# Two attentions on one core: outputs kept with tokens in rows, and turned by DMA in the last stage

## The chip, the core and the metric

The kernel runs on one core of a Trainium2 chip. The core has five engines with a queue of instructions each: TensorE (PE in the profile, with its weight loads as PEld), VectorE (DVE), ScalarE (ACT), GpSimd (POOL) and SyncE (SP), which here issues every DMA. Each queue is worked in order; semaphores tie the queues together. The metric is the device time of one execution in microseconds, the median of several runs.

## The reference

Two attention layers over 2048 tokens of width 1024 with 32 heads of 32 stand side by side; their outputs are concatenated. Cut to what is computed:

```python
def _A_ref(x, wq, wk, wv, wo, beta):          # four segments of 512 tokens
    for s in range(N):
        p = _softmax(q_s @ k_s.T * scale + mask)
        a_dot = p @ v_s
        a_mem = phi(q_s) @ M / (phi(q_s) @ z + 1e-6)
        outs.append(g * a_mem + (1 - g) * a_dot)
        M, z = M + phi(k_s).T @ v_s, z + phi(k_s).sum(tokens)
    return concat(outs) @ wo
def _B_ref(x, wqkv, w_phi, wo):               # linear attention, all tokens
    phi(t) = concat(softmax(t @ w_phi), softmax(-t @ w_phi))
    o = phi(q) @ (phi(k).T @ v) / (phi(q) @ phi(k).sum(tokens) + 1e-6)
    return o @ wo
return concatenate([_A_ref(...), _B_ref(...)], axis=-1)
```

All of it is in 32-bit floats, so the kernel splits most operands into a high and a low half float ("halves") and multiplies three times: high x high, high x low, low x high.

## The kernel before

**Stages.** First comes attention A in 32 units (`attend`, `produce`), one for each segment and group of four heads; B's folded weights are prepared beside it. Then come B's keys and values (eight pairs of 128 tokens, by Strassen's scheme with seven products in place of eight), then B's queries with B's output projection (`project`, 16 blocks of 128 tokens), and last A's output projection, again by Strassen's scheme: eight passes `c`, each for the token blocks c and c + 8.

**A's outputs.** A unit ends with `osum`, a tile with 128 tokens in rows and, for each of four token blocks, 128 columns of four heads. TensorE turns the four 128x128 blocks (line 1108) into a bank of PSUM, ScalarE copies them to `oT` (line 676), and SP stores `oT` to the DRAM tensor `oa_d` (line 1110). So `oa_d` holds features in rows and tokens in columns. `oT` is also the name under which folded weights are kept on their way to DRAM (lines 534, 535 and 1135).

**The last stage.** A pass loads its two token blocks from `oa_d` (line 1686; tiles `e`, or S9 for pass 0), forms four sums and differences on VectorE (line 1692), and makes halves of seven operands: A11, A12, S1, S2, S4, S3, A22 (lines 455 and 457). The halves go to `ot`, `pt` and `h3` tiles, for pass 0 (`own`) to S15 and S8. They are the stationary operand of the matmuls (line 1725), 12 for each of the seven products, so 84 to a pass; the moving operand is one of seven forms of the output weights (S0 to S3, S10, S13, S14). Results leave through ScalarE (line 1742), VectorE (line 1749) and SP (line 1751); pass 0 keeps them in S12. The last product of the last pass leaves in two halves of its width (lines 1773, 1775 and 1778).

**Buffers by name.** S4 to S7 hold the halves of B's output weights (`bo`: S4 and S5 for the first 512 columns, S6 and S7 for the second) until the last `project` (line 428 with `misc<-S,ot`). The DMA transposes already there are at line 904 (keys of A) and line 1653 (B's queries: four for each block of 128 tokens, 128x1024 half floats each).

**The order.** Nothing is issued as written. Every operation goes into a graph with an expected duration, a priority and the operations it depends on, and `Graph.run` fills the five queues from it, always taking the operation with the best priority among those that could start by its own model of time. `nudge` shifts priorities by a pseudo-random amount that a table, `NUDGE`, sets for each stretch of 60 operations (`G.places` counts them). Where the model sees TensorE idle for long it puts in dummy matmuls (`fill`, line 386).

Of the kernel before, what the change touches and what calls it, by code (L numbers as in the profile page):

```python
# [8 lines left out]
F32 = mybir.dt.float32  # L9
F32R = mybir.dt.float32r  # L10
F16 = mybir.dt.float16
# [31 lines left out]
         ((3, 0, "subtract"), 3, 2), ((2, 3, "subtract"), 2, 6))  # L43
EUP = 2.0 ** 15
STRETCH, REACH = 60, (0.3, 0.7, 1.5, 3.0)
NUDGE = {0: 820989, 2: 102852, 3: 529656, 4: 266905, 5: 924189, 6: 435410, 9: 911235, 12: 450738, 13: 124130, 14: 669972,
# [15 lines left out]


def view(t, off, ap):
# [41 lines left out]
class Graph:  # L106
# [37 lines left out]
    def op(self, eng, dur, fn, r=(), w=(), prio=0, lat=0.0, short=False, port=False, need=(), kb=256, free=False):  # L144
        o = Op()
        o.short, o.port = short, port or eng == "POOL"
        o.eng, o.dur, o.fn, o.prio, o.lat, o.kb = eng, dur, fn, (prio, len(self.ops)), lat, kb
        o.banks = []
        ends, starts = set(), set()
        for b in need:  # L150
            if b.prev[0] is not None:
                ends.update(b.prev[0].ops)
        for write, accs in ((0, r), (1, w)):
            for acc in accs:
                b, key = acc if isinstance(acc, tuple) else (acc, None)
                b = b.of if type(b) is Part else b
                old, last, opened = b.prev
                if old is not None:
                    ends.update(old.ops)
                if not b.ops and last is not None:  # L160
                    starts.add(last.ops[0])
                if opened is not None:
                    starts.add(opened)
                for k in (list(b.writer) if key is None else [key, None]):
                    if k in b.writer:
                        ends.add(b.writer[k])
                if write:
                    for k in (list(b.readers) if key is None else [key, None]):
                        ends.update(b.readers.pop(k, ()) if k == key or key is None else b.readers.get(k, ()))
                    if key is None:  # L170
                        b.writer.clear()
                    b.writer[key] = o
                else:
                    b.readers.setdefault(key, []).append(o)
                b.ops.append(o)
                if b.kind is not None and b not in o.banks:
                    o.banks.append(b)
                    b.left += 1
        ends.discard(o)
        o.deps = [(d, 0) for d in ends] + [(d, 1) for d in starts - ends if d is not o]  # L180
        o.base, o.at = prio, None if free else self.places
        self.places += not free
        last = self.ops[-1] if self.ops else o
        if o.eng == "PE" and (last.eng, last.base, last.fn.__code__, last.banks) == (o.eng, prio, fn.__code__, o.banks):
            o.at = last.at
        o.prio = (prio + (0.0 if o.at is None else nudge(o.at)), len(self.ops))
        self.ops.append(o)
        return o
# [121 lines left out]
def tile_kernel(ctx: ExitStack, tc: tile.TileContext, ax, aw, awv, awo, beta, bx, bwqk, bwv, bphi, bwo, out):  # L310
# [97 lines left out]
    def bank(tag, shape, line=None):  # L408
        b = G.bank(tag, shape, F32, line or tag)
        psums.add(b)  # L410
        return b
# [263 lines left out]
    def copy(dst, src):  # L675
        return lambda: nc.scalar.activation(dst(), src(), AF.Copy)
# [241 lines left out]
    def attend(u):  # L918
# [5 lines left out]
        def pe(dur, fn, **kw):  # L924
            op(PE, dur, fn, prio=P, **kw)

        def act(dur, fn, **kw):
            op(ACT, dur, fn, prio=P, **kw)
# [173 lines left out]
        if s > 0:  # L1102
            pool(1.23, lambda: nc.gpsimd.tensor_tensor(
                osum(), osum(), amem().rearrange("p c h d -> p c (h d)"), op=OP.add), r=[amem, osum], w=[osum])
        oT = G.buf("a", [128, 4, 128], F32, "oT", 1)
        po = bank("misc", [128, 4, 128], "output")
        for i in range(4):
            pe(0.112, lambda i=i: nc.tensor.transpose(po()[:, i, :], osum()[:, i, :], ident), r=[osum], w=[po], need=[oT])
        act(0.48, copy(oT, po), r=[po], w=[oT])
        op(SP, 0.6, lambda: nc.sync.dma_start(oa_d[4 * s:4 * s + 4, :, g, :].rearrange("c p t -> p c t"), oT()),  # L1110
           r=[oT], w=[(osc, u)], prio=P, lat=1.5)

    wfb, xfb, bob = (G.fixed(t) for t in (wf_d, xf_d, bo_d))
    lanes = [G.fixed(None) for _ in range(2)]
# [561 lines left out]
    for c in range(NT // 2):  # L1676
# [18 lines left out]
        def half(t, h, o=0):  # L1695
            return lambda: t()[:, o + h]
# [5 lines left out]
        if own:  # L1702
            fb = [G.buf("slot", [128, 4096], F16, s) for s in ("S15", "S8")]
            at2 = [(fb[j // 4], j % 4) for j in range(7)]
        else:
            o2 = [G.buf("b", [128, 2112], F16, "ot", 4) for _ in range(2)]
            p2 = G.buf("b", [128, 2112 - 64], F16, "pt", 3)
            hx = G.buf("slot", [128, 2048], F16, "h3", 2)
            at2 = [(o2[0], 0), (o2[0], 1), (o2[1], 0), (o2[1], 1), (p2, 0), (p2, 1), (hx, 0)]

        def pick(t, i, a):
            return t()[:, 1024 * i + 512 * a:1024 * i + 512 * a + 512].rearrange("p (b c) -> p b c", c=128)

        for (f, src, k), (t, i) in zip((("A11", A0, 0), ("A12", A0, 1), ("S1", ss, 0), ("S2", ss, 1), ("S4", ss, 3),
                                        ("S3", ss, 2), ("A22", A1, 1)), at2):
            form[f] = (t, i, lambda a, t=t, i=i: pick(t, i, a))
            hl = [(t, (i, a), lambda a=a, t=t, i=i: pick(t, i, a)) for a in range(2)]
            sk = (src, k) if src is ss else (src, int(f == "A22"))
            halves(*hl, (sk, half(src, k, off if f == "A22" else 0)), (oscs, 0, lambda: osc2[:, 0]), 512, P)

        def mult(ps, f, w, start):
            t, i, v = form[f]
# [4 lines left out]
                        stop=(n == 3 and a == 1), skip_group_check=True),  # L1727
                       r=[(t, (i, a)), (wform[w], (b, n))], w=[ps], prio=P)

        kept = []  # L1730
        if own:
            ks = G.buf("slot", [128, 4, 512], F32, "S12")

        def keep(ps, tag, bufs):
            if own:
                t, i = ks, len(kept)
                kept.append(i)
                v = lambda: ks()[:, i]
            else:
                t, i = G.buf("b" if tag == "ez" else "stage", [128, 512], F32, tag, bufs), None  # L1740
                v = t
            op(ACT, 0.587, lambda: nc.scalar.activation(v(), ps(), AF.Copy, scale=wsc[:, 2, 1, 0:1]),
               r=[ps, (wscs, (2, 1))], w=[(t, i)], prio=P)
            return (t, i), v
# [74 lines left out]
```

## Time and profile before

| what | value |
|---|---|
| median of 3 runs | 1662.68 us (1659.73 to 1662.96) |
| the profiled execution | 1660.7 us |
| its span, first to last instruction | 1658.7 us |
| mean granted TensorE clock | 0.999 |
| attention A | to about 887 us |
| B's keys and values | about 887 to 1200 us |
| B's queries and `project` | about 1200 to 1509.7 us |
| A's output projection, passes 0 to 7 | 1509.7 to 1658.7 us |

The page's first row gives the busy time of each engine, and its second part the same in 40 slices of the span. A view by stretch gives, for each window, the length, the busy time of each engine with its number of instructions, the granted TensorE clock, the share of time the 16 DMA engines worked, and GB/s. A group of instructions is one line, engine and operation with its tiles, its count, busy time, mean duration in ns, and the idle time of its engine just before. A row of the timeline is start, duration, engine, line, operation, tiles, and count; SPq is SP's queue issuing DMAs. Rows of one line or tile end with the shortest, median and longest duration in ns. A row of waits reads: who waited, for whom, us in total, times, longest.

### The profile page before, as it was taken

The numbers are of one execution on the slowest core, as the hardware profiler recorded it, in microseconds if no ns is written. First come the engines' busy times: TensorE is split into PE (matmuls) and PEld (weight loads), VectorE is DVE, ScalarE is ACT, GpSimd is POOL, SyncE is SP. The second block draws the span as 40 slices with busy tenths as digits, with TensorE's granted clock in tenths as the row PEclk, the third lists the DMA queues.
The fourth block names the chain that finished last, engine by engine and source line by source line (L and its number), as shares of the span: only waits on it lengthen the run. The fifth ranks groups of instructions, "written<-read, shape, count | busy, mean of one in ns | idle before, by whom it ended". The sixth has DMA issues, their size and how long they took to land.

```text
span 1658.7 us, 35573 instructions
## 1 busy us (share of the span) xinstructions
PE 1639.3 (99%) x12922; PEld 967.3 (58%) x12922; DVE 1356.5 (82%) x3213; ACT 1110.3 (67%) x2044; POOL 1058.9 (64%) x1394
## 2 busy tenths in 40 slices
PE   9999999999999999999999999999999999999999
PEld 7666667667676666766754444445544444444444
DVE  6999989899887888897877898979996786975441
ACT  8799779869787777687865767645656464444331
POOL 4967577577787887967875444646799897640000
PEclk9999999999999999999999999999999999999999
DMA  7855556789556573766576364276466665763311
GB/s 239 239 139 154 155 161 171 202 206 248 110 158 163 136 186 88 196 193 181 164 215 228 121 222 147 96 272 241 169 152 143 174 174 152 221 149 133 121 57 64
DMA packets 265599, 279.68 MB, mean 169 GB/s; under 512 B 162768, under 2 KB 216016, under 8 KB 256848
## 3 DMA queue, kind: packets, MB, share of 16 engines
q1 hardware_dynamic: 265424, 277.42, 58.1%
q8 instruction: 101, 1.65, 0.4%
q14 instruction: 74, 0.61, 0.1%
HBM read 143.34 MB, written 85.00 MB: 138 GB/s over the span
## 4 chain that ended last, share of the span: by engine, by line
PE 76%; DVE 10%; POOL 6%; ACT 4%; issue 3%; DMA 0%; SPq 0%; POOLq 0%; ACTq 0%; DVEq 0%
PE proj L428 25%; PE proj L624 13%; PE misc L428 8%; PE proj L1725 5%; PE s L1040 3%; PE s L947 3%; PE pv L1076 3%; PE s L624 3%; PE s L1725 2%; PE misc L624 2%; PE misc L1725 1%; POOL e L1630 1%; DVE mx L1326 1%; PE pv L1661 1%; DVE ph L1047 1%
## 5 line engine op out<-in xcount | busy, mean ns | idle before, releaser
L428 PE MATMUL proj<-S,S 128*128 128x512 f16 (+1 forms) x2304 | 493.9, 343 | 0.8 <-DVE ph L1047 0.4
L428 PEld LDWEIGHTS <-S 128*128 128x128 f16 x3072 | 288.9, 98 | 158.0 <-ACT S L455 0.7
L624 PE MATMUL proj<-S,S 128*128 128x512 f16 x1488 | 342.8, 379 | 7.0 <-ACT cs L630 6.0
L624 PEld LDWEIGHTS <-S 128*128 128x128 f16 x1968 | 186.9, 98 | 220.3 <-issue 8.6
L1053 POOL TENSOR_SCALAR_AFFINE_SELECT ph<-ph 128x256 f16<-128x256 f16 (+1 forms) x448 | 194.3, 457 | 108.2 <-DVE ph L1047 91.3
L1047 DVE SCALAR_TENSOR_TENSOR ph<-s,ph 128x512 f16<-128x512 f32 x320 | 208.6, 684 | 49.4 <-ACT ph L1046 45.0
L953 DVE CUSTOM_DVE_ANT_0 s<-s,causal 128x384 f32<-128x384 f32 (+3 forms) x512 | 241.4, 511 | 7.4 <-PE s L947 4.8
L1046 ACT ACTIVATE ph<-s 128x512 f16<-128x512 f32 x320 | 184.8, 645 | 0.7
L428 PE MATMUL misc<-S,ot 128*128 128x512 f16 x768 | 171.0, 379 | 0.0
L1333 ACT ACTIVATE e<-e,sk 128x256 f32<-128x256 f32 x256 | 114.2, 497 | 60.7 <-DVE e L1330 38.9
L428 PEld LDWEIGHTS <-ot 128*128 128x128 f16 x768 | 73.9, 98 | 88.3
L1044 ACT ACTIVATE s<-s,bdl 128x512 f32<-128x512 f32 x160 | 105.6, 701 | 19.6 <-PE s L1040 19.6
L1044 ACT ACTIVATE s<-s,bd 128x512 f32<-128x512 f32 x160 | 102.9, 687 | 18.6 <-PE s L1040 16.9
L1040 PE MATMUL s<-S 104*128 104x512 f16 (+3 forms) x512 | 113.2, 299 | 0.3 <-ACT S L977 0.3
L947 PE MATMUL s<-S 96*128 96x512 f16 (+3 forms) x512 | 112.0, 299 | 0.7 <-DVE dm L1000 0.3
L428 PE MATMUL proj<-wv,S 128*128 128x256 f16 x768 | 101.1, 272 | 0.0
L1076 PEld LDWEIGHTS <-ph 128*128 128x128 f16 x2560 | 88.9, 96 | 19.1 <-POOL ph L1053 0.9
L1630 POOL TENSOR_TENSOR e<-e,zb 128x512 f32<-128x512 f32 x64 | 84.9, 1341 | 16.2 <-DVE r L1336 13.2
L1076 PE MATMUL pv<-vl,ph 128*128 128x66 f16 (+1 forms) x2560 | 92.5, 184 | 0.1
L1336 DVE TENSOR_REDUCE r<-e 128x32 f32<-128x1024 f32 x64 | 76.7, 1207 | 12.2 <-ACT e L1333 11.9
L624 PE MATMUL s<-S,S 128*128 128x512 f16 x324 | 78.6, 379 | 0.4 <-DVE S L457 0.4
L953 DVE DVE_READ_ACCUMULATOR2_ANT mt<- 128x1 f32 x512 | 72.7, 142 | 0.0
(376 smaller groups left out, 3302.4 us busy)
## 6 DMA issues: line engine op xcount, KB each, us to landing
S<-h SPq DMA_DIRECT2D x192, 128.0 KB
S<-wf_d SPq DMA_DIRECT2D x21, 1024.0 KB
st<-bwqk SPq DMA_DIRECT2D x56, 256.0 KB
wf_d<-fo SPq DMA_DIRECT2D x48, 256.0 KB
out<-os SPq DMA_DIRECT2D x38, 256.0 KB
wf_d<-oT SPq DMA_DIRECT2D x36, 256.0 KB
S<-xf_d SPq DMA_DIRECT2D x9, 1024.0 KB
S<-aw SPq DMA_DIRECT2D x16, 512.0 KB
```

Source lines behind the costliest of these rows:

```text
L428: op(PE, dur, lambda c=c, a=a, b=b, lv=lv, rv=rv: nc.tensor.matmul(pv(), lv(), rv(), start=(c == 0 and a + b == 0), stop=(c == n - 1 and a ...
L624: op(PE, 0.2165, lambda n=n, a=a, b=b, lv=lv, rv=rv: nc.tensor.matmul(ps(), lv(), rv(), start=(start and n == 0 and a + b == 0), stop=(n = ...
L947: nc.tensor.matmul(ps()[:, o:o + 128 * i + 128], st()[0:96, 0, h, 128 * i:128 * i + 128], st()[0:96, 1, h, 0:128 * i + 128], start=True, s ...
L953: dve({128: 0.216, 256: 0.381, 384: 0.6, 512: 0.648}[n], lambda h=h, i=i, o=o, n=n: nc.vector.tensor_tensor_reduce(ps()[:, o:o + n], ps()[ ...
L1040: nc.tensor.matmul(ps()[:, o:o + n], st()[0:104, 1, h, 128 * j:128 * j + 128], st()[0:104, 0, h, 128 * j:512], start=True, stop=True)
L1044: act(0.571, lambda: nc.scalar.activation(ps(), ps(), AF.Exp, bias=0.0, scale=bd()[:, 4, i2, 0:1]), r=[(bd, i2)], w=[ps])
L1046: act(0.478, lambda: nc.scalar.activation(ph()[:, 0], ps(), AF.Copy, scale=2.0 ** 14), r=[ps], w=[(ph, 0)])
L1047: dve(0.6, lambda: nc.vector.scalar_tensor_tensor(ph()[:, 1], ps(), 2.0 ** 14, ph()[:, 0], op0=OP.mult, op1=OP.subtract), r=[ps, (ph, 0)], ...
L1053: nc.gpsimd.affine_select(pd, pd, pattern=[[0, n], [1, 128]], compare_op=OP.is_ge, fill=0.0, base=0, channel_multiplier=-1)
L1076: nc.tensor.matmul(ps()[:, i, n0:n1], ph()[:, a, o:o + 128], vl()[:, j, h4 + h, n0:n1], start=(i == 0 and a == 0), stop=(j == min(i, 2)), ...
L1333: op(ACT, 0.41, lambda i=i: nc.scalar.activation(e()[:, 4 * i:4 * i + 4], e()[:, 4 * i:4 * i + 4], AF.Exp, bias=0.0, scale=sk()[:, i:i + 1 ...
L1725: op(PE, 0.2165, lambda n=n, a=a, b=b: nc.tensor.matmul(ps(), v(a)[:, n, :], wform[w]()[:, b, n, :], start=(start and n == 0 and a + b == ...
```

## The change

`oa_d` now holds A's outputs as the unit leaves them, tokens in rows. The four transposes, the bank of PSUM, and the copy to `oT` are gone, and SP stores `osum` itself. In the last stage the loads, the sums and differences, and the halves have the same shapes as before, with tokens in rows; then a DMA transpose turns each operand's halves (128 x 1024 half floats, high and low together), and the matmuls read the turned tiles. There are seven for each pass, 56 in all. The turned tiles are S12 and two `h3` tiles for pass 0, and by turns S6 and S7 (odd passes) and S4 and S5 (even passes) for the others, four operands in the first and three in the second. Since S12 is taken, pass 0 keeps its results in `cs` tiles. `G.places += 5` keeps the count of operations for the nudges; the transposes are not counted. The table `NUDGE` is another one, from its third entry on.

```diff
-NUDGE = {0: 820989, 2: 102852, 3: 529656, 4: 266905, 5: 924189, 6: 435410, 9: 911235, 12: 450738, 13: 124130, 14: 669972,
+NUDGE = {0: 820989, 2: 102852, 3: 733272, 5: 984992, 6: 222437, 8: 980432, 9: 306119, 10: 758093, 11: 242234, 12: 151133, 13:
...
-        oT = G.buf("a", [128, 4, 128], F32, "oT", 1)
-        po = bank("misc", [128, 4, 128], "output")
-        for i in range(4):
-            pe(0.112, lambda i=i: nc.tensor.transpose(po()[:, i, :], osum()[:, i, :], ident), r=[osum], w=[po], need=[oT])
-        act(0.48, copy(oT, po), r=[po], w=[oT])
-        op(SP, 0.6, lambda: nc.sync.dma_start(oa_d[4 * s:4 * s + 4, :, g, :].rearrange("c p t -> p c t"), oT()),
-           r=[oT], w=[(osc, u)], prio=P, lat=1.5)
+        G.places += 5
+        op(SP, 0.6, lambda: nc.sync.dma_start(oa_d[4 * s:4 * s + 4, :, g, :].rearrange("c p t -> p c t"), osum()),
+           r=[osum], w=[(osc, u)], prio=P, lat=1.5)
...
+        turned = [("S12", 4), ("h3", 2), ("h3", 1)] if own else [(f"S{4 + 2 * (c % 2)}", 4), (f"S{5 + 2 * (c % 2)}", 3)]
+        turned = [(b, k) for b, n in ((G.buf("slot", [128, 2 if t == "h3" else 4, 2, 4, 128], F16, t, 2 if t == "h3" else 1), n)
+                                      for t, n in turned) for k in range(n)]
...
-            form[f] = (t, i, lambda a, t=t, i=i: pick(t, i, a))
+            form[f] = (b, o, lambda a, b=b, o=o: b()[:, o, a])
             hl = [(t, (i, a), lambda a=a, t=t, i=i: pick(t, i, a)) for a in range(2)]
             sk = (src, k) if src is ss else (src, int(f == "A22"))
             halves(*hl, (sk, half(src, k, off if f == "A22" else 0)), (oscs, 0, lambda: osc2[:, 0]), 512, P)
+            op(SP, 1.24, lambda t=t, i=i, b=b, o=o: nc.sync.dma_start_transpose(
+                b()[:, o].rearrange("p a g t -> p (a g) t"), t()[:, 1024 * i:1024 * i + 1024]),
+               r=[x[:2] for x in hl], w=[(b, (o, a)) for a in range(2)], prio=P, lat=2.0, kb=256, free=True)
...
-            if own:
-                t, i = ks, len(kept)
-                kept.append(i)
-                v = lambda: ks()[:, i]
-            else:
-                t, i = G.buf("b" if tag == "ez" else "stage", [128, 512], F32, tag, bufs), None
-                v = t
+            t, i = G.buf(*CS) if own else G.buf("b" if tag == "ez" else "stage", [128, 512], F32, tag, bufs), None
+            v = t
```

What stands in the queues now, at three places. The first is TensorE in the attention: before, around the first unit's transposes (the rows that begin with L1108; `S_440` are A's key and query weights, `S_130` a unit's stacked keys and queries).

```order
L1013 LDWEIGHTS pkt
L1013 MATMUL misc<-vl_122,pkt 128x132
L1108 MATMUL misc<-ident,osum 128x128 x4
L428 LDWEIGHTS S_440
L428 MATMUL proj<-S_826,S_440 128x512
L428 LDWEIGHTS S_440
L428 MATMUL proj<-S_826,S_440 128x512
```

After the change no such row is left on TensorE, 32 times four transposes fewer, and SP's queue has the store of `osum` in the place of that of `oT`, between the copies of weights and halves of the units that follow:

```order
L885 DMA S_138<-h_1407 32x4x512 x2
L1136 DMA wf_d<-oT 1024x1x128
L1111 DMA oa_d<-osum 128x4x128
L1136 DMA wf_d<-fo 1024x1x128
L885 DMA S_138<-h_1407 32x4x512 x3
```

What moved: the four transposes went from TensorE, and the store waits for `osum` rather than for ScalarE's copy.

The second place is SP's queue at the entry to the last stage after the change. `out<-os` are the last results of `project`, S_21426 and S_21449 the turned tiles of pass 2 (in S4 and S5), S_21466 and S_21504 those of pass 1 (in S6 and S7), `cs` the results of pass 0.

```order
L1548 DMA out<-os 128x512
L1724 DMA_TRANSPOSE S_21426<-ot 128x8x128
L1548 DMA out<-os 128x512
L1724 DMA_TRANSPOSE S_21426<-ot 128x8x128
L1724 DMA_TRANSPOSE S_21449<-pt 128x8x128 x2
L1724 DMA_TRANSPOSE S_21466<-ot 128x8x128
L1548 DMA out<-os 128x512
L1724 DMA_TRANSPOSE S_21466<-ot 128x8x128 x3
L1724 DMA_TRANSPOSE S_21504<-pt 128x8x128
L1548 DMA out<-os 128x512
L1724 DMA_TRANSPOSE S_21504<-pt 128x8x128
L1724 DMA_TRANSPOSE S_21426<-ot 128x8x128 x2
```

New here are twelve transposes between the stores, with those for pass 2 ahead of those for pass 1. On TensorE, 17 of pass 0's 84 matmuls now stand in front of the last matmul of `project`, against one before.

The third place is SP's queue in a later pass. Before, it holds only the loads of `e` and the stores:

```order
L1751 DMA out<-st 128x512
L1686 DMA e<-oa_d 128x1024
L1751 DMA out<-st 128x512
L1751 DMA out<-ez 128x512
L1751 DMA out<-os 128x512
```

After, the stores of the passes ahead stand between the transposes of passes 4 and 5 (S_21839 and S_21905 are pass 4's turned tiles, S_21967 four operands of pass 5):

```order
L1724 DMA_TRANSPOSE S_21839<-ot 128x8x128 x4
L1750 DMA out<-st 128x512
L1750 DMA out<-ez 128x512
L1687 DMA e<-oa_d 128x1024
L1724 DMA_TRANSPOSE S_21905<-pt 128x8x128 x2
L1750 DMA out<-os 128x512
L1724 DMA_TRANSPOSE S_21905<-h_21675 128x8x128
L1750 DMA out<-st 128x512
L1724 DMA_TRANSPOSE S_21967<-ot 128x8x128 x3
```

What moved: seven transposes for a pass were put between the stores, so that a transpose can stand behind a store whose result is not there yet.

More of the change, by code (lines that the diff above doesn't have):

```diff
@@ L1709, in tile_kernel @@
             at2 = [(o2[0], 0), (o2[0], 1), (o2[1], 0), (o2[1], 1), (p2, 0), (p2, 1), (hx, 0)]
+        turned = [("S12", 4), ("h3", 2), ("h3", 1)] if own else [(f"S{4 + 2 * (c % 2)}", 4), (f"S{5 + 2 * (c % 2)}", 3)]
+        turned = [(b, k) for b, n in ((G.buf("slot", [128, 2 if t == "h3" else 4, 2, 4, 128], F16, t, 2 if t == "h3" else 1), n)
+                                      for t, n in turned) for k in range(n)]
         def pick(t, i, a):
             return t()[:, 1024 * i + 512 * a:1024 * i + 512 * a + 512].rearrange("p (b c) -> p b c", c=128)
-        for (f, src, k), (t, i) in zip((("A11", A0, 0), ("A12", A0, 1), ("S1", ss, 0), ("S2", ss, 1), ("S4", ss, 3),
-                                        ("S3", ss, 2), ("A22", A1, 1)), at2):
-            form[f] = (t, i, lambda a, t=t, i=i: pick(t, i, a))
+        for (f, src, k), (t, i), (b, o) in zip((("A11", A0, 0), ("A12", A0, 1), ("S1", ss, 0), ("S2", ss, 1), ("S4", ss, 3),
+                                                ("S3", ss, 2), ("A22", A1, 1)), at2, turned):
+            form[f] = (b, o, lambda a, b=b, o=o: b()[:, o, a])
             hl = [(t, (i, a), lambda a=a, t=t, i=i: pick(t, i, a)) for a in range(2)]
@@ L1728, in mult @@
                        r=[(t, (i, a)), (wform[w], (b, n))], w=[ps], prio=P)
-        kept = []
-        if own:
-            ks = G.buf("slot", [128, 4, 512], F32, "S12")
         def keep(ps, tag, bufs):
-            if own:
-                t, i = ks, len(kept)
-                kept.append(i)
-                v = lambda: ks()[:, i]
-            else:
-                t, i = G.buf("b" if tag == "ez" else "stage", [128, 512], F32, tag, bufs), None
-                v = t
+            t, i = G.buf(*CS) if own else G.buf("b" if tag == "ez" else "stage", [128, 512], F32, tag, bufs), None
+            v = t
             op(ACT, 0.587, lambda: nc.scalar.activation(v(), ps(), AF.Copy, scale=wsc[:, 2, 1, 0:1]),
```

35 rows, old and new, of the table NUDGE are left out of this document.

## The prediction

> **What bounds the kernel now.** I read the page's busy row first, then the busy times by stretch, then TensorE's own rows.
>
> ```profile
> PE 1639.3 (99%) x12922; PEld 967.3 (58%) x12922; DVE 1356.5 (82%) x3213; ACT 1110.3 (67%) x2044; POOL 1058.9 (64%) x1394
> core 0: us, PE busy (x) PEld busy (x) DVE busy (x) ACT busy (x) POOL busy (x), PEclk, DMA share, GB/s
> 150.00:300.00 150.00, 149.78 (x1467) 105.65 (x1466) 140.60 (x421) 125.57 (x231) 101.56 (x165) 1.00 0.64 174
> 985.00:1190.00 205.00, 201.71 (x1435) 103.22 (x1433) 183.92 (x320) 129.11 (x272) 112.07 (x101) 1.00 0.51 184
> 1190.00:1215.00 25.00, 22.17 (x143) 11.39 (x144) 25.00 (x45) 12.94 (x30) 21.37 (x28) 1.00 0.63 179
> 1300.00:1480.00 180.00, 180.00 (x1193) 85.37 (x1192) 149.31 (x222) 92.66 (x163) 137.59 (x155) 1.00 0.64 169
> 1509.70:1658.70 149.00, 145.01 (x672) 65.56 (x670) 52.38 (x76) 45.52 (x69) 0.00 (x0) 0.99 0.21 78
> ```
>
> TensorE is busy in all but 1658.7 - 1639.3 = 19.4 us of the span. In the attention (row 150 to 300) it has 0.2 us idle in 150, in the query half of B (1300 to 1480) none, in the last stage (1509.7 to 1658.7) 4.0 us, which is the tail behind its last matmul. So a us of TensorE work taken out is a us off the end, as long as nothing else falls behind in the same stretch. The only stretch where it waits for its own needs is B's keys and the handover to the queries: 3.3 us in 985 to 1190 and 2.8 us in 1190 to 1215. The granted clock is 1.00 or 0.99 everywhere and plays no part.
>
> **What the change takes from TensorE.** The four transposes of each of 32 attention units go.
>
> ```profile
> L1108 PE MATMUL misc<-ident,osum 128*128 128x128 f32 x128 | 19.3, 274 | 0.0
> 94.81 0.70 PE L1013 MATMUL misc<-vl,pkt 128*128 128x132 f16 x9
> 95.35 0.60 PE L1108 MATMUL misc<-ident,osum 128*128 128x128 f32 x4
> 95.78 1.24 PE L428 MATMUL proj<-S,S 128*128 128x512 f16 x5
> ...
> 145.44 0.66 PE L1108 MATMUL misc<-ident,osum 128*128 128x128 f32 x4
> 145.94 1.07 PE L994 MATMUL misc<-mem,pq 128*128 128x132 f32 x8
> ...
> 885.41 0.60 PE L1108 MATMUL misc<-ident,osum 128*128 128x128 f32 x4
> 885.85 0.81 PE L624 MATMUL s<-S,S 128*128 128x512 f16 x3
> ```
>
> The group row shows 19.3 us busy and 274 ns each, but that is not what they cost: the next matmul starts while the last transpose still counts as busy. From the start of a run of four to the start of what follows are 95.78 - 95.35 = 0.43 us, 145.94 - 145.44 = 0.50 and 885.85 - 885.41 = 0.44. I take 0.44, the case that stands at both ends of the stage: **32 x 0.44 = 14.1 us**. The bounds are 32 x 0.43 = 13.8 and 32 x 0.50 = 16.0; the 19.3 of the group row would need every run to stand alone. None of the 128 stands next to idle time (the last column is 0.0), so nothing hides behind them, and all of them lie before 887 us, where TensorE hardly waits.
>
> **What it takes from ScalarE.** One copy per unit out of PSUM.
>
> ```profile
> L676 ACT ACTIVATE oT<-misc x32: 575/597/713, 96.0 to 886.0; 128x512 f32<-128x512 f32 x32
> L1110 SPq DMA_DIRECT2D oa_d<-oT x32: 370/394/1367, 97.3 to 886.7; - x32
> PE proj L624 <- ACT cs L630: 6.0, 4, 2.4
> ```
>
> 32 x 0.597 = 19.1 us of ScalarE work go. TensorE's only sizeable wait for ScalarE is the 6.0 us at line 624, after the last of these copies, so I count the relief at nothing. The store to DRAM has the same shape and size as before and starts two steps sooner. `osum` is now held until its store has landed; it is written again a unit later, 887 / 32 = 28 us, against a store whose issue takes 0.39 us and whose landing, by the 2.1 us found below for another DMA, takes a few. That cover is far too long to lose.
>
> **What it adds: 56 DMA transposes in the last stage**, seven for each of eight passes, all issued by SP. The trace has the same operation at the same size, 128x1024 half floats, in B's query half.
>
> ```profile
> 1364.34 5.41 SPq L1653 DMA_TRANSPOSE pt<-kls  x4
> q1 hardware_dynamic: 4368, 1.31, 62.1%
> out<-os SPq DMA_DIRECT2D x1, 256.0 KB
> pt<-kls SPq DMA_TRANSPOSE x4
> 1483.72 5.59 SPq L1653 DMA_TRANSPOSE pt<-kls  x4
> 1489.41 1.02 SPq L1686 DMA_DIRECT2D e<-oa_d  x2
> 1490.52 0.38 SPq L1547 DMA_DIRECT2D out<-os  x1
> 1491.42 0.69 DVE L1692 TENSOR_TENSOR kls<-e 128x512 f32<-128x512 f32 x1 [4.86 <-DMA pt<-kls]
> 1525.21 5.18 PE proj L1725 x24
> ```
>
> The second to fourth lines are the DMA queue from 1364 to 1374 us, the last is from the chain that ended last. SP issues four transposes in 5.41 and 5.59 us, so 1.40 each. In that 10 us window the DMA engines worked 6.2 us for four transposes and one store: at most 1.55 us each. The last of the group issued by 1489.31 had landed by 1491.42, 2.1 us later. A pass of the last stage is 84 matmuls of 5.18 / 24 = 0.216, so 18.1 us. Against that SP has 7 x 1.40, two loads in 1.02 and four stores of 0.38: 12.3 us; the DMA engines have 7 x 1.55 and what they do now, 0.21 x 18.1 = 3.8: 14.7 us. Both fit, so **in the steady passes I count nothing**. Turned tiles alternate between two pairs of buffers, so the transposes of a pass run while the pass ahead multiplies. If that cover were gone, the price is what SP or the DMA engines need beyond 18.1 us, times seven passes.
>
> The Trainium skill (VectorE: DVE Perf Modes) speaks against the change: its section The three transpose paths gives 390 ns for a 128x128 block of bf16 on TensorE and 1309 ns by DMA, and its Rules for kernel authors advise TensorE where the result may go to PSUM. Eight blocks at 1309 ns would be an estimated 10.5 us for one of these DMAs, 73 us for a pass, and some 2030 us for the kernel; the trace does not agree, with eight blocks every 1.40 us, so that figure can't be a rate here.
>
> **The entry to the last stage** is the one place with a new wait. Pass 1 turns into S6 and S7, which hold half of B's output weights until the last `project` matmul; pass 2 turns into S4 and S5, free 24 matmuls (5.2 us) earlier. In the new order 17 of pass 0's 84 matmuls stand ahead of that last `project`, and 67 behind it: 67 x 0.216 = 14.5 us of work whose seven transposes were issued before. A first turned form is ready 1.40 + 2.1 = 3.5 us after its buffer is free, and all seven after 7 x 1.40 + 2.1 = 11.9. Queued on SP behind a waiting transpose are stores of `project` and the loads of later passes; TensorE waits for neither soon. So nothing here too; if the cover were gone altogether, 11.9 us once. The seven transposes of pass 0 fall where TensorE idles 0.0 of 180 us, with the DMA share at 0.64.
>
> **The tail.** Before, two half-width copies and two stores follow the last matmul (4.0 us). Now one full-width DVE operation and one 256 KB store do. The DVE operation at this width took 0.75 us where the half took 0.48:
>
> ```profile
> 1652.16 0.75 DVE L1749 SCALAR_TENSOR_TENSOR ez<-s,wsc,ez 128x512 f32<-128x512 f32 x1 [1.78 <-PE s L1725]
> 1652.94 0.33 SPq L1751 DMA_DIRECT2D out<-ez  x1
> 1654.75 0.48 DVE L1775 TENSOR_SCALAR os<-proj,wsc 128x256 f32<-128x256 f32 x1 [1.84 <-PE proj L1725]
> 1655.26 0.89 SPq L1778 DMA_DIRECT2D out<-os  x2
> ```
>
> 0.27 more on DVE, 0.89 - 0.33 = 0.56 less on SP, and twice the data behind it: between -0.3 and +0.5 us. I take 0.
>
> **The order chosen anew** moves nearly every instruction on every engine by some places. Its price can't be read from a row; its bounds can. What TensorE waits for inside the program, and an order can touch, is 3.3 + 2.8 us in the two stretches above and some 1.5 us in small pieces elsewhere (0.2 us in each 150 of the attention): 7.6. I let it move from -7.6 (all gone) to +7.6 (doubled) and take 0, since the fillers that the planner puts into gaps of TensorE number 11 after the attention in both orders.
>
> **Sum.** The profiled execution took 1660.7 us with a span of 1658.7: 1660.7 - 14.1 = 1646.6. The median of the runs, 1662.68, is 2.0 above it; I go half way, **1647.6 us**, 0.9% less than the median.
>
> **Rivals.**
> *The new order opens gaps.* By the bound above 1646.6 + 7.6 = 1654.2. For it: DVE is at 25.00 of 25 in 1190 to 1215, where a small reordering costs TensorE us. Against: the removed work isn't there. Chance 0.15; the gaps closing instead, 1639.0, 0.08.
> *DVE becomes the bound of the attention.* It is busy 140.60 of 150 us, 94%, and every probability tile passes through it; with 14.1 / 887 = 1.6% less TensorE time it would be at 95%. If DVE's waits for others already fill the other 6%, the stage stays as long and the time is 1660.7. Against: in these 150 us TensorE waited 0.2 us, so DVE still runs ahead. Chance 0.06, no change.
> *The transposes starve the last stage*, the slower side. An issue was not always 1.40 us:
>
> ```profile
> 1204.43 17.22 SPq L1653 DMA_TRANSPOSE pt<-kls  x6
> L1653 SPq DMA_TRANSPOSE pt<-kls x64: 1231/1257/3529, 1201.1 to 1488.0; - x64
> SPq L1653 <- ACT kls L1648: 22.4, 12, 6.8
> ```
>
> Six in 17.22 us are 2.87 each, and one alone took 3.5. At 2.87 a pass needs 7 x 2.87 + 2.5 = 22.6 us of SP, 4.5 too many; over seven passes 31 us, so 1646.6 + 31 = 1678. It decides from (18.1 - 2.5) / 7 = 2.2 us a transpose on. Against: SP waited 22.4 us for the tiles it was to turn (third line), so the 2.87 hold waiting for sources, and the two groups whose sources were there took 1.40. Chance 0.06. (The Trainium skill's DMA figure, above, would be this rival at its worst; the trace leaves it under 0.01 of the 0.06.)
> *The change doesn't do what it says:* on TensorE it does, 128 transposes are gone from its list and nothing is put in their place.
>
> **How the numbers follow.** Forecast case 0.65, between 1640 and 1654. About 0.2% (3.3 us) is what a measurement of this kernel can tell from no change, so faster means under 1659.4. Forecast, gaps and closed gaps are faster: 0.65 + 0.15 + 0.08 = 0.88, less 0.01 for gaps so large that nothing is left: 0.87. No change is DVE's 0.06 and that 0.01: 0.07. Slower is starving, 0.06. The range goes from 1639 (gaps closed) to 1656 (gaps doubled, plus the 2.0 of the median); it leaves out DVE, starving and the ends, below 0.2.
>
> **What would show it.** Right: no transposes on TensorE before 887 us, TensorE's total of idle time still near 19 us, the attention ending some 14 us sooner, the last stage again 145 us of TensorE without a wait for DMA. Wrong: TensorE's first matmuls of a pass waiting for a DMA into S4 to S7; SP waiting in the last stage with turned tiles outstanding; DVE above 97% in the attention with TensorE idle; more than 7 us idle between 985 and 1215.

## The result, and the profile after

| | median | lowest to highest | runs |
|---|---|---|---|
| before | 1661.62 us | 1659.73 to 1662.96 | 4 |
| after | 1670.92 us | 1669.27 to 1671.44 | 4 |

The changed kernel is slower: the ratio is 1.0055, with an interval of 1.0043 to 1.0067. The prediction said 1647.6 us and was wrong in sign.

First the busy row of the page of after, then its busy times by stretch, with the same columns as those of before.

```profile
PE 1630.0 (98%) x12784; PEld 952.7 (57%) x12784; DVE 1380.3 (83%) x3213; ACT 1094.2 (66%) x2012; POOL 1063.2 (64%) x1394
```

```profile
150.00:300.00 150.00, 149.36 (x1443) 103.24 (x1442) 143.12 (x419) 128.67 (x233) 105.66 (x168) 1.00 0.63 173
450.00:600.00 150.00, 147.23 (x1383) 98.26 (x1381) 128.00 (x383) 111.93 (x205) 124.10 (x173) 1.00 0.55 149
985.00:1190.00 205.00, 199.51 (x1435) 102.64 (x1434) 186.30 (x315) 128.68 (x270) 112.90 (x102) 1.00 0.51 186
1190.00:1215.00 25.00, 23.37 (x137) 11.70 (x136) 23.94 (x43) 15.82 (x34) 20.34 (x27) 1.00 0.57 165
1300.00:1480.00 180.00, 176.24 (x1172) 83.33 (x1170) 146.56 (x215) 92.19 (x166) 137.34 (x150) 1.00 0.70 172
1509.70:1667.50 157.80, 153.66 (x712) 69.37 (x709) 61.32 (x90) 50.91 (x78) 0.00 (x0) 1.00 0.70 171
```

TensorE has less to do (1630.0 against 1639.3 us), but the span is 1667.5 us, so its idle time went from 19.4 to 37.5. The idle time is spread over the program: 2.8 us in 450 to 600, 5.5 in 985 to 1190, 3.8 in 1300 to 1480, where before had none at all. Between 985 and 1215 it is 5.5 + 1.6 = 7.1 us, just over the 7 that the prediction had named as a sign of being wrong. In the last stage, 157.80 - 153.66 = 4.1 us are idle, the tail, as before. The groups of TensorE's waits in after are line, what it waited for, us in total, times, and the longest:

```profile
PE proj L629 <- ACT cs L635: 5.1, 7, 1.0
PE proj L629 <- DVE cs L639: 3.3, 4, 1.3
PE misc L980 <- DVE rowt L975: 2.8, 2, 2.4
PE pv L1662 <- DMA pt<-kls: 2.4, 3, 1.1
PE misc L1263 <- DVE ident L349: 2.2, 1, 2.2
PE pv L1081 <- POOL ph L1058: 1.9, 5, 0.9
```

No single wait took the place of the transposes. There are many short ones, for VectorE, ScalarE, GpSimd and a DMA in turn. Where the time went is seen best from the ends of the stages, read from the last matmul of each (us; the last column is the run e10, described below: the whole change in the order of before, with the store early):

| last matmul of | before | after | difference | e10 |
|---|---|---|---|---|
| attention (`pv` of A) | 879.5 | 874.1 | -5.4 | 877.0 |
| B's keys (`kv`) | 1178.5 | 1182.2 | +3.7 | 1175.6 |
| B's queries (`pv` of B) | 1495.5 | 1504.7 | +9.2 | 1491.3 |
| `project` | 1509.9 | 1521.8 | +11.9 | 1506.5 |
| the last stage | 1654.7 | 1663.6 | +8.9 | 1651.3 |

The attention ends 5.4 us sooner, not 14. Then 9.1 us are lost in B's keys and 5.5 in the queries, stages from which the change takes nothing that TensorE did. To tell waiting from work, here are these three stages by busy time, first of before, then of after, then of e10:

```profile
0.00:879.50 879.50, 871.94 (x8048) 596.22 (x8049) 765.09 (x2270) 700.52 (x1271) 654.54 (x973) 1.00 0.65 177
879.50:1178.50 299.00, 296.77 (x2050) 149.33 (x2047) 262.65 (x451) 189.00 (x390) 158.14 (x149) 1.00 0.53 190
1178.50:1495.50 317.00, 311.39 (x2091) 149.70 (x2091) 263.65 (x399) 167.93 (x304) 246.24 (x273) 1.00 0.64 167
```

```profile
0.00:874.10 874.10, 857.48 (x7898) 579.85 (x7899) 773.41 (x2269) 683.97 (x1239) 654.37 (x972) 1.00 0.65 177
874.10:1182.20 308.10, 299.96 (x2058) 150.56 (x2057) 275.19 (x455) 192.36 (x395) 160.16 (x150) 1.00 0.51 186
1182.20:1504.70 322.50, 313.87 (x2098) 150.66 (x2098) 265.43 (x394) 164.07 (x298) 248.62 (x272) 1.00 0.69 168
```

```profile
0.00:877.00 877.00, 862.33 (x7924) 582.35 (x7925) 762.33 (x2270) 685.67 (x1240) 654.14 (x973) 1.00 0.64 177
877.00:1175.60 298.60, 296.37 (x2046) 149.05 (x2043) 262.68 (x452) 188.52 (x389) 158.21 (x149) 1.00 0.53 191
1175.60:1491.30 315.70, 310.38 (x2086) 149.35 (x2087) 260.18 (x393) 166.42 (x301) 245.96 (x273) 1.00 0.67 170
```

A stage's length less TensorE's busy time is its idle time there: 7.6, 2.2 and 5.6 us before, 16.6, 8.1 and 8.6 after. So TensorE waits longer in all three stages, the attention above all. The rest of the 9.1 in B's keys is work that moved: twelve matmuls (`misc<-S,S`, some 2.6 us at 0.216) stand ahead of the attention's last `pv` before and behind it after, and by as much the attention seems to end sooner than it does.

In B's keys of after, 7.1 of the 8.1 us of waiting name VectorE. The largest groups between 874 and 1182 us:

```profile
PE proj L629 <- DVE cs L639: 2.2, 3, 1.3
PE pv L576 <- DVE xt L574: 1.9, 2, 1.5
PE kv L1481 <- DVE pt L1474: 1.4, 3, 0.5
PE fill L391 <- DVE za L1490: 1.4, 1, 1.4
```

The +11.9 at `project` holds 16 more matmuls of pass 0 that now stand ahead of it (3.5 us at 0.216, ten of them already in the queries), which the last stage gets back.

The last stage is as the prediction described it. TensorE's only wait from 1505 us on, and SP's waits and queue there (the rows with times are start, duration, queue, line, operation):

```profile
PE proj L1732 <- ACT st L1741: 0.2, 1, 0.2
```

```profile
SPq L1724 <- PE s L1732: 9.4, 4, 4.0
```

```profile
1558.61 2.80 SPq L1724 DMA_TRANSPOSE S<-ot  x2
1561.50 0.52 SPq L1750 DMA_DIRECT2D out<-st  x1
1562.63 2.62 SPq L1724 DMA_TRANSPOSE S<-pt  x2
1565.30 1.32 SPq L1724 DMA_TRANSPOSE S<-h  x1
```

Two transposes take 2.80 and 2.62 us, 1.3 to 1.4 each, and SP has time to wait for the matmuls that free the buffers (9.4 us in this group, the largest): the transposes run ahead of TensorE. The DMA share is 0.70 where 0.81 had been worked out (14.7 of 18.1). The tail is 1667.5 - 1663.6 = 3.9 us, against 4.0.

### The profile page after: what moved, and what is told of

Same layout as the page of the kernel before. It is cut to its first block, busy times and chain, and to the rows that moved or that the text cites. A ratio compares the mean times of both kernels' runs of the same rounds, so it can differ in the third digit from the quotient of the medians.

```text
span 1667.5 us, 35341 instructions
## 1 busy us (share of the span) xinstructions
PE 1630.0 (98%) x12784; PEld 952.7 (57%) x12784; DVE 1380.3 (83%) x3213; ACT 1094.2 (66%) x2012; POOL 1063.2 (64%) x1394
## 4 chain that ended last, share of the span: by engine, by line
PE 44%; DVE 12%; POOL 8%; ACT 5%; issue 3%; DMA 1%; SPq 0%; ACTq 0%; DVEq 0%; POOLq 0%
PE proj L629 10%; PE proj L433 9%; PE misc L433 5%; PE proj L1732 5%; PE s L629 3%; PE s L1732 2%; POOL e L1631 2%; PE s L1045 1%; PE misc L629 1%; POOL e L1643 1%; PE s L952 1%; PE pv L1081 1%; DVE mx L1327 1%; PE misc L1732 1%; DVE r L1337 1%
## 5 line engine op out<-in xcount | busy, mean ns | idle before, releaser
L433 PEld LDWEIGHTS <-S 128*128 128x128 f16 x3072 | 288.5, 98 | 156.4 <-issue 1.3
L629 PE MATMUL proj<-S,S 128*128 128x512 f16 x1488 | 344.2, 379 | 10.4 <-ACT cs L635 5.1
L629 PEld LDWEIGHTS <-S 128*128 128x128 f16 x1968 | 187.4, 98 | 226.7 <-issue 15.5
L1631 POOL TENSOR_TENSOR e<-e,zb 128x512 f32<-128x512 f32 x64 | 90.2, 1425 | 39.0 <-DVE r L1337 37.6
L1732 PEld LDWEIGHTS <-S 128*128 128x128 f16 x636 | 62.1, 98 | 75.2 <-issue 0.5
L1732 PE MATMUL proj<-S,S 128*128 128x512 f16 x360 | 82.6, 379 | 0.2 <-ACT st L1741 0.2
```

Of the source, the lines that this page charges most:

```text
L433: op(PE, dur, lambda c=c, a=a, b=b, lv=lv, rv=rv: nc.tensor.matmul(pv(), lv(), rv(), start=(c == 0 and a + b == 0), stop=(c == n - 1 and a ...
L629: op(PE, 0.2165, lambda n=n, a=a, b=b, lv=lv, rv=rv: nc.tensor.matmul(ps(), lv(), rv(), start=(start and n == 0 and a + b == 0), stop=(n = ...
L1631: op(POOL, 1.23, lambda a=a, h0=h0, e=e: nc.gpsimd.tensor_tensor(e()[:, 8 * a:8 * a + 8], e()[:, 8 * a:8 * a + 8], zv()[:, h0:h0 + 8], op= ...
L1732: op(PE, 0.2165, lambda n=n, a=a, b=b: nc.tensor.matmul(ps(), v(a)[:, n, :], wform[w]()[:, b, n, :], start=(start and n == 0 and a + b == ...
```

## The experiments

Four theories stood at the start or came up.
- **A, the order:** TensorE's 14 us are there to be had, and the order chosen anew gives them back.
- **B, another engine:** VectorE or ScalarE bounds the attention, so TensorE's saving returns as waits in any order.
- **C, the last stage:** the transposing DMAs hold something up.
- **D, the store** (found in e3): `osum` is free only when its store has landed, and VectorE waits for it.

Runs are named by the first part of their labels.

**The tables exchanged (e1, e2).** The kernel before with the new table, and the changed kernel with the old one:

```diff
-NUDGE = {0: 820989, 2: 102852, 3: 529656, 4: 266905, ...
+NUDGE = {0: 820989, 2: 102852, 3: 733272, 5: 984992, ...
```

> The kernel before with the new table alone, nothing else changed. Theory A in its strong form (the new table is a bad one for this program): 1675 to 1690. If instead a table only fits the one program that it was made for, this lies above before by as much as any table not made for it, perhaps 5 to 25 us. Theories B and C: the table matters little, 1658 to 1666.

> The changed kernel with the table of before. The transposes no longer take room in the plan, so its order drifts from that of before after the first unit. Theory A: the old table is not fitted to this program either, 1650 to 1675, and the spread of this run and the changed kernel shows what a table is worth. Theories B and C: within 4 us of the changed kernel, 1667 to 1675.

The first took 1722.08 us, 1.0363 [1.0347, 1.0378] of before; the second 1699.17 us, 1.0228 [1.0213, 1.0243]. Each table is good for its own program alone: under the table fitted to the other, the kernel before is 60 us slower and the changed one 28. A difference of 9 us between two fitted kernels is small beside what the table decides.

**No table at all (e5, e6):**

```diff
-NUDGE = {0: 820989, ...
+NUDGE = {}
```

> The kernel before with an empty table: the planner's own order. Theory A (a table is worth tens of us and fits one program alone): 1685 to 1725. If the table matters little: 1661 to 1670.

> The changed kernel with an empty table. Neither plain order was fitted to anything, so the difference from the plain kernel before is the change with the luck of one order each. Theory A: 14 us under the plain kernel before, give or take the spread of unfitted orders, some 15 us. Theory B: the same as it or slower.

Before took 1737.30 us (1.045 [1.0434, 1.0465]), the changed kernel 1705.84 (1.0261 [1.0245, 1.0276]). Without tables the changed program is 31.5 us faster. The tables are worth 1737.30 - 1661 = 76 us to the kernel before, and 1705.84 - 1670.92 = 35 to the changed one. This speaks against B and C, but weakly, since two orders without a table can differ by more than the change.

**The order held (e3, e4).** To keep the order of before on every engine, the planner is given operations that emit nothing, with the durations of the four transposes and the copy. In e3 that is the whole edit, so its last stage multiplies operands that nobody turned; e4 is the full change with the order of before up to the last stage. The pairs e7 and e8, e9 and e10 below differ in the same way.

```diff
-            pe(0.112, lambda i=i: nc.tensor.transpose(po()[:, i, :], osum()[:, i, :], ident), r=[osum], w=[po], need=[oT])
-        act(0.48, copy(oT, po), r=[po], w=[oT])
-        op(SP, 0.6, lambda: nc.sync.dma_start(oa_d[...], oT()),
+            pe(0.112, lambda i=i: None, r=[osum], w=[po], need=[oT])
+        act(0.48, lambda: None, r=[po], w=[oT])
+        op(SP, 0.6, lambda: nc.sync.dma_start(oa_d[...], osum()),
```

> The kernel before with the attention part of the change alone: the planner still plans the four transposes and the copy, with their durations, but they issue nothing, so TensorE, DVE, ACT, POOL and SP keep the order of before, less 128 transposes and 32 copies; osum is stored. The last stage multiplies operands that were not turned. Theory A (the new order costs some 23 us, the removal itself is worth its 14.1): 1661.6 - 14.1 = 1647.5, at most 1651. Theory B (without TensorE's transposes another engine sets the pace of the attention, so the 14 us are lost whatever the order): 1658 to 1662. Theory C (the DMA transposes hold up the rest of the kernel): 1647.5, as A.

> The whole change with the table of before and the same placeholders in the plan, so that all engines keep the order of before up to the last stage's first work; the last stage is that of the change, with 56 DMA transposes. Theory A: as the attention part alone, 1647.5, within 2 us. Theory B: 1658 to 1671. Theory C: 10 to 23 us over the attention part alone, so 1658 to 1671, lost after the first turned tiles of the last stage.

They took 1675.45 us (1.0084 [1.0069, 1.0099]) and 1678.74 us (1.0098 [1.0081, 1.0115]): slower than before, with 128 transposes fewer in the same order. A as it stood had failed, and both times lie above B's ranges too (1658 to 1662 and 1658 to 1671). The groups of VectorE's waits in e3 and its timeline (start, duration, engine, line; in brackets how long the engine sat idle, and for what) name it:

```profile
DVE osum L1099 <- DMA oa_d<-osum: 17.3, 5, 5.7
```

```profile
568.01 1.64 DVE L1099 TENSOR_TENSOR osum<-oall,rd 128x512 f32<-128x512 f32 x1
...
592.40 0.61 SPq L1110 DMA_DIRECT2D oa_d<-osum  x1
...
598.43 0.69 DVE L1099 TENSOR_TENSOR osum<-oall,rd 128x512 f32<-128x512 f32 x1 [5.24 <-DMA oa_d<-osum]
...
602.04 0.43 PE L975 MATMUL misc<-rowt 128*128 128x128 f16 x4 [4.78 <-DVE rowt L970]
```

One unit's `osum` is written from 568.01 on; GpSimd's add to it, from 569.8, takes 1.26, so it could be stored from about 571 on. Its store stands where the copied `oT` was stored before, and issues at 592.40, 24 us later. The next unit's `osum` is due at about 593; VectorE stops there for 5.24 us, with all that is queued behind it, and TensorE then stands for 4.78. Before, `osum` was released by the transposes, which sat at such late places without harm, since they read `osum` at once. A store reads it until it lands, 6 us after its issue here. So the trace shows the wait of theory D; what it costs can be told only by moving the store.

**The store on ScalarE's queue (e7, e8),** at the place of the copy, so a step sooner:

```diff
-        act(0.48, lambda: None, r=[po], w=[oT])
-        op(SP, 0.6, lambda: nc.sync.dma_start(oa_d[...], osum()),
+        act(0.48, lambda: nc.scalar.dma_start(oa_d[...], osum()), r=[po], w=[oT])
+        op(SP, 0.6, lambda: None,
```

> As the attention part alone in the order of before, but the store of osum is issued by ScalarE's queue at the place where the copy to oT stood, not by SP at its old late place, so that osum is free long before VectorE writes it again. The last stage multiplies operands that were not turned. Theory A (the 14.1 us come off the end once nothing new is waited for; the 14.6 us lost in the run before were VectorE waiting for the late store): 1660.8 - 14.1 = 1646.7, within 3 us, and no wait of VectorE for a DMA of osum. Theory B (another engine sets the attention's pace): 1656 or more, with TensorE waiting in many short pieces and no long ones.

> The whole change in the order of before, the store of osum issued by ScalarE's queue. Theory A: 1646.7 and what the entry to the last stage adds, which the two runs before put at 3.3 us: 1647 to 1651. Theory B: 1656 or more. Theory C (the DMA transposes hold up the last stage): 10 us or more above the attention part alone.

1671.75 us (1.0055 [1.004, 1.007]) and 1672.83 us (1.0061 [1.0043, 1.008]). A miss as a repair: the copy's place is as late as the transposes', and VectorE still waits 13.5 us in five places:

```profile
DVE osum L1099 <- DMA oa_d<-osum: 13.5, 5, 5.7
```

But the pair speaks against C: the 56 transposes and all that the last stage does with them cost 1.1 us between them (3.3 in the pair before), where C asked for 10 or more.

**The store early (e9, e10),** on SP right behind the last operation that writes `osum`; the order of the other four engines stays that of before (in e10 up to the last stage). The 64 transposes in the second expectation are a slip: e10 has the 56 of the changed kernel.

```diff
+        made = osum.writer[None]
+        early = op(SP, 0.0, lambda: nc.sync.dma_start(oa_d[...], osum()), prio=-50, kb=0, free=True)
+        early.deps = [(made, 0)]
...
-        act(0.48, lambda: nc.scalar.dma_start(oa_d[...], osum()), r=[po], w=[oT])
+        act(0.48, lambda: None, r=[po], w=[oT])
```

> The kernel before without its 128 transposes of osum and their 32 copies; every TensorE, VectorE, ScalarE and GpSimd instruction that is left stands in the order of before, and the store of osum is now put on SP right behind the add that makes osum, not at the place where the copy was. The last stage multiplies operands that nobody turned, so this output leaves out that turning. Theory A (the loss is a matter of order and of places: with before's order kept and the store early, TensorE's 14.1 us come off the end): 1647 us, 1644 to 1651, and VectorE's groups name no wait for the DMA of osum any more (13.5 us where ScalarE issued it late). Theory B (another engine has become the bound of the attention, so that TensorE's saving returns as waits whatever the order): no less than 1656 us, with TensorE idle over 30 us in its span.

> The whole change with the correct output: as the run beside it (order of before, the store of osum right behind its last add), with the last stage's operands turned by 64 DMA transposes. Theory A: 1 to 3 us over the run beside it, 1645 to 1654 us, and so below the kernel before and below the changed kernel. Theory C (the transposing DMAs hold up the last stage): over 5 us above the run beside it. Theory B: no less than 1656 us, as the run beside it.

They took 1656.70 us (0.9964 [0.9951, 0.9977]) and 1657.08 us (0.9964 [0.995, 0.9979], 5 runs of each against 9 of before at 1662.55). **e10, the whole change, is faster than both kernels:** by 0.36% than before, by 0.9% than the changed kernel (0.9964 against 1.0055). It has the instructions of the changed kernel and ten more dummy matmuls, in another order:

```profile
PE 1629.1 (98%) x12794; PEld 953.1 (58%) x12794; DVE 1354.1 (82%) x3213; ACT 1095.1 (66%) x2012; POOL 1058.3 (64%) x1394
```

(This is the busy row of e10's page; VectorE does the same 3213 instructions as in after in 26 us less.) So 0.9% of 1662, some 15 us, is what the new order costs against the old one; the two profiled spans are 12.1 us apart.

This shows D: in e9 VectorE's waits name no DMA for `osum` any more, and 1675.45 has become 1656.70. A's number was not reached, though: 5.9 us came off, not 14.1. TensorE's matmuls stand in one order in before and e9, so the times from one start to the next can be compared pair by pair: at the 32 places where transposes were, the time falls by 13.9 us together; at 43 others it grows by 13.5 together, at 23 others it falls by 3.7, and the remaining 12695 pairs change by 0.6. The sum, -3.5, is the difference of the two profiled spans (1655.2 against 1658.7). Of the growth, 11.4 lie in the attention. But 1.3 of these stand at 9 us, where nothing had been taken out yet (the first transposes stood at 95 us): a run of matmuls is quicker there in e9's profile, and the next one, which waits for ScalarE, starts at 9.5 us in both. The falls hold 1.3 for the same reason, so 10.1 us of growth are left for the change. The windows of the attention, summed, of before and then of e9:

```profile
sum 880.00, PE 872.44 PEld 596.42 DVE 765.59 ACT 700.92 POOL 654.62; mean PE 145.41 PEld 99.40 DVE 127.60 ACT 116.82 POOL 109.10
```

```profile
sum 880.00, PE 864.63 PEld 583.30 DVE 765.79 ACT 687.20 POOL 656.23; mean PE 144.10 PEld 97.22 DVE 127.63 ACT 114.53 POOL 109.37
```

TensorE's idle time in these 880 us goes from 7.6 to 15.4. The groups of its waits, three of before, then the same three of e9:

```profile
PE misc L439 <- ACT S L497: 0.6, 1, 0.6
PE misc L975 <- DVE rowt L970: 0.6, 1, 0.6
PE s L1040 <- ACT S L977: 0.3, 1, 0.3
```

```profile
PE misc L448 <- ACT S L506: 3.3, 2, 1.9
PE misc L984 <- DVE rowt L979: 1.7, 4, 0.6
PE s L1049 <- ACT S L986: 1.4, 2, 1.0
```

The 0.6 of the first row before and the 1.9 of the first row of e9 are the place at 9.5 us. Without it the three waits go from nothing, 0.6 and 0.3 to 1.4, 1.7 and 1.4, behind ScalarE and VectorE in turn. TensorE got ahead of hand-overs that were just in time. The longest of them, 1.4 us at 295 us, may have another cause: ScalarE waits there for a load that had not landed (3.8 us between 290 and 300 us, 1.8 before), and on SP's queue e9's early store stands right ahead of that load (issues at 285.21 and 286.13). Whether the store held the load up was not tried.

**VectorE relieved (e11).** Is it VectorE's load that sends the 8 us back? This is e9 with a cheaper operation in the place of the one that makes `osum`:

```diff
-        dve(0.6, lambda: nc.vector.tensor_tensor(
-            osum()..., oall()[:, :, :, 0:32], rd()[...], op=OP.mult), r=[oall, rd], w=[osum], port=True)
+        dve(0.6, lambda: nc.vector.tensor_scalar(
+            out=osum()..., in0=oall()[:, :, :, 0:32], scalar1=1e-12, scalar2=None, op0=OP.mult),
+            r=[oall, rd], w=[osum], port=True)
```

> The run with the early store and without the last stage's turning (1656.7 us against 1662.6 for the kernel before beside it), with VectorE relieved at one place: the 32 multiplications of the attention's sums by their row factors (osum <- oall, rd; 815 ns each in the profile of before, 26.1 us) become multiplications by a constant, which read one tile instead of two; the order on every engine stays as it was. The output leaves out the row factors. Theory B in its weaker form (VectorE's load in the attention is what returns 8 of the 14 us): the time follows VectorE's relief, 5 us or more below the kernel with the factors, if VectorE's osum group falls by 10 us or more. Theory A (the hand-overs of this order were set with the transposes in it, and the waits that come back end with loads, ScalarE and VectorE alike): within 2.5 us of the kernel with the factors.

It took 1652.83 us, 0.9942 [0.9926, 0.9959], against 0.9964 [0.9951, 0.9977] for e9. The groups of that line, of e9 and of this run:

```profile
L1108 DVE TENSOR_TENSOR osum<-oall,rd 128x512 f32<-128x512 f32 x32 | 26.1, 816 | 1.0 <-POOL rd L1106 0.6 <-issue 0.2
```

```profile
L1108 DVE TENSOR_SCALAR osum<-oall 128x512 f32<-128x512 f32 x32 | 16.2, 505 | 0.0
```

VectorE lost 9.9 us of work and the kernel some 0.22%, 3.7 us. That lies between the bounds of the two theories, the two intervals overlap, and VectorE's relief was just under the 10 us that B's bound asked for, so the share of VectorE in the 8 us stays open. The edit also takes away a wait: the new operation doesn't read `rd`, which GpSimd makes (0.6 us in the first row, nothing in the second). That VectorE's load in the attention is worth something to the end is likely by this run, but not shown.

## Why the prediction was wrong, step by step

- **The transposes' time, 32 x 0.44 = 14.1 us of TensorE:** right. The 32 places gave 13.9.
- **"So a us of TensorE work taken out is a us off the end":** this failed. With the order kept and the store placed well, 5.9 of 14.1 us came off. The prediction saw that TensorE never waited and took that for slack in the others. TensorE at 99% says that the hand-overs come before it needs them, not how long before; here it got ahead of them by little at many places (34 of the 43 places that grew lie in the attention, and 28 of these grew by less than 0.5 us). The condition in the same sentence, "as long as nothing else falls behind in the same stretch", is the one that did not hold, and no row had been looked up for it.
- **"`osum` is now held until its store has landed ... That cover is far too long to lose":** wrong in the working, and by luck not a part of this result. The 28 us are from one write to the next; what counts is from the place of the store in the order to the next write. In the order of before that is next to nothing for some units, and cost about 19 us (1675.45 against 1656.70). The changed kernel's planner put the stores early, and its VectorE waits for no such DMA. Whether having to place them made its order worse was not tried.
- **"The order chosen anew ... -7.6 to +7.6 and take 0":** this is the term that turned the sign. It was taken at 0 and bounded at half its size: between e10 and the changed kernel the order is worth some 15 us. In the two profiles, TensorE waits 16.6 - 14.7 = 1.9 us more in the attention of after than in that of e10, 5.9 more in B's keys and 3.3 more in the queries, 11.1 of the 12.1 us between the spans. "0.2 us in each 150 of the attention" is the reading of one row; the attention of before has 7.6 us of idle time, 4.2 of them in its first 94 us. And the bound was built on the waits that are left in a fitted order, which says nothing of another order: with no table at all the same program was 76 us slower. The count of fillers, on which 0 was taken, had no bearing; the traces hold 16 behind the attention's last `pv` before and 20 after, not 11 and 11.
- **The 56 transposes, nothing:** right, 0.4 us between e9 and e10, 1.1 and 3.3 between the others. 1.3 to 1.4 us an issue held.
- **The entry to the last stage and the tail, nothing:** right (0.2 us of waiting, 3.9 us of tail).
- **The rivals.** "The new order opens gaps" was the right one, at 1654.2 instead of 1670.9, since it had the same small bound. "DVE becomes the bound" did not occur as written, since the time moved with the order alone; how little slack VectorE has is what e11 leaves open. "The transposes starve the last stage", on which all of the slower side's chance stood, did not occur.

The result is then: -14.1 us from the transposes, about +8 that return in the old order, most of it because the other engines' hand-overs come in time for the slower TensorE only, and about +15 from the new order. That makes 9, as measured (9.3). The 8 and the 15 are differences between runs; what lies behind the 15 stays open. One lead is VectorE: with the same 3213 instructions it is busy 26 us longer in after than in e10. In B's keys it is busy 275.19 us against 262.68 with three instructions more, and TensorE's waits there name it; the 24 operations `pt<-e,pt` of that stage, for one, take 24.5 us against 21.4. No run tests whether this causes the loss or goes along with it, nor which rule or number in the planner brings it about.

## What to carry to other kernels

Where an order was fitted to a kernel, a change to any part of it must be judged in two steps: in the old order, with what is removed left as a blank, and then in the new one; here the two had opposite signs, and the old order with one store moved beat both kernels. An engine that is busy 99% of the time tells how much it waits now, not how early its inputs come: before counting a us of its work as a us of time, look at the gap between each input's arrival and its use. When a buffer's reader changes from an engine to a DMA, count the cover from where the DMA stands in its queue to the next write, not from write to write.

## What was not expected of the hardware

After a stop, TensorE can run at half speed for a while. The windows of about 3.5 us behind one stop of 2.3 us in e9 and one of 4.8 us in e3 (columns as above; the granted clock is the third number from the end):

```profile
1186.30:1190.00 3.70, 3.52 (x9) 1.31 (x9) 3.70 (x7) 3.38 (x11) 3.58 (x4) 0.54 0.17 20
1190.00:1194.00 4.00, 4.00 (x21) 1.78 (x19) 3.91 (x9) 2.57 (x7) 2.79 (x8) 1.00 0.87 277
```

```profile
602.00:605.50 3.50, 3.46 (x14) 1.65 (x15) 2.84 (x13) 1.22 (x3) 3.50 (x5) 0.54 0.05 7
```

The clock was 0.54 for some 3.5 us and 1.00 after that, so by the first row such a stop costs about 3.7 x 0.46 = 1.7 us more than the wait shown. It does not always: behind a stop as long (2.25 us, before the matmul at 1190.43), before had 1.00:

```profile
1190.30:1194.00 3.70, 3.57 (x17) 1.66 (x17) 3.70 (x7) 3.70 (x12) 3.62 (x4) 1.00 0.19 24
```

The Trainium skill, TensorE: Matmul & The Clock Gate, section Part 1: The HAM clock gate, describes this: the clock halves after an idle window of about 3.4 us and comes back after a busy one, and the windows run freely. The length of the slow piece agrees. That a stop of 2.3 us was enough once does not agree with its advice to keep gaps below 3.4 us; the measurement decides.
